# The filter's features for all positions first, then transformed by the forward's tiles, in a long convolution with a mixture of experts

## The chip, the cores and the metric

The kernel runs on one core of a Trainium2 chip. The metric is the device time of one execution in microseconds (us), as the median of several runs. TensorE (PE) multiplies matrices into PSUM, VectorE (DVE), ScalarE (ACT) and GpSimd (POOL) do the elementwise work, and SyncE (SP) issues nearly all loads and stores. Each engine works through its own instructions in the order in which the program wrote them.

## The reference

Four sequences of 11456 positions with 128 channels are convolved with a long filter, gated, and sent through a mixture of eight experts:

```python
h_mlp = np.maximum(pos_emb @ w1, 0.0) @ w2          # (11456, 64) -> (11456, 128)
h_filt = h_mlp * np.exp(-0.01 * pos)[:, None]
u = x * v
L = 2 * S
y = np.fft.irfft(np.fft.rfft(u, n=L, axis=1) * np.fft.rfft(h_filt, n=L, axis=0)[None], n=L, axis=1)[:, :S]
x = (x * y).reshape(B * S, D)
logits = x @ w_gate + modality_bias[modality_id]
e_idx = np.argmax(logits, axis=1)                   # one expert of 8 for each token
out[mask] = gate_w[mask, None] * (np.maximum(x[mask] @ w1[e], 0.0) @ w2[e])
```

Only `pos_emb`, `w1` and `w2` enter the filter, which is the same for all four sequences.

## The kernel before

The Fourier transforms are products with constant matrices. A position is split into a block (2 of them), a place n and its mirror (the two "ways"), and one of N2 = 64 remainders. A forward transform first makes the even and the odd part of the two ways, multiplies them with `fwd` (90 columns, over n), and then, in the middle stage, with matrices `c_to` over the 64 remainders. The middle stage runs over NM = 23 groups g of up to four of the 90 frequencies.

The first stage (0 to about 75 us) has 16 quarters q of two kinds. For sequence 0, `load(q)` fetches 512 KB of x (`xd`) and 512 KB of v, `product(q)` on DVE multiplies them and makes the even and odd parts (three instructions, in place in v's buffer), and `transform(q)` multiplies with `fwd`: two halves of 16 matmuls, each half into one of two PSUM pairs, from which ACT copies into the tile `A`. For the filter, `load(q)` fetches 256 KB of `pos_emb`, `hidden(q)` multiplies with w1 (four matmuls), DVE applies the relu and the window, and `transform(q)` multiplies at once with `whole`, a matrix that does even, odd and `fwd` together (four matmuls of 128x180); ACT copies to the tile `B`, which shares its memory with work buffers.

The middle stage of sequence 0 has more to do than the others, since the filter is finished in it: `turn(g)` transposes four 128x128 tiles of `B` on TensorE, and ACT copies them out; `analysis(g)` multiplies with `c_to`; `second(g)` multiplies with w2; `keep(g)` stores the spectrum of the filter for the sequences that follow. `swap(g)` (ACT), `spectrum(g)` (PE, then DVE and POOL) and `inverse(g)` (PE, ACT) belong to the sequence. Then follow the inverse transform, routing, and the experts, which the change leaves alone.

The order on every engine is written by the class `Timeline`: each piece has a time (a number without unit), and all pieces are issued in the order of time, place and rank. The tables `FOUT`, `FIRST` and `MID0` give the offset of each piece: `turn:-3` means that `turn(g)` stands three groups ahead of the sequence's `spectrum(g)`. A load waits until its buffer is free, and SP waits with it; so whatever is behind it on SP waits too. `ring_of` lists the buffers of each name.

Lines in the profile: L506 and L509 are `hidden`, L519 and L523 the filter's `transform`, L471, L474 and L475 `product`, L486 and L489 the sequence's `transform`, L561 and L562 `turn`, L570 and L574 `analysis`, L584 to L590 `second`, L599 and L600 `swap`, L617 to L644 `spectrum`, L658 and L662 `inverse`.

Of the kernel before, what the change touches and what calls it, by code (L numbers as in the profile page):

```python
# [91 lines left out]
def shape_constants():  # L92
# [6 lines left out]
    whole = np.zeros((2, 64, N1, 2))  # L99
    whole[:, :HALF, :, 0], whole[0, :HALF, :, 1], whole[1, :HALF, :, 1] = even, odd, -odd  # L100
# [22 lines left out]
    win = win.reshape(2, 64, 2, N2).transpose(2, 1, 3, 0)  # L123
# [18 lines left out]
        "c_inv": f(inv.reshape(N1, D)), "c_to": f(to), "c_back": f(back), "c_early": f(np.concatenate([win.reshape(D, 2 * N2), whole.reshape(D, 2 * N1)], 1)),  # L142
# [36 lines left out]
def hyena_moe_kernel(ctx: ExitStack, tc: tile.TileContext, a: dict, out: bass.AP,  # L179
# [184 lines left out]
    with ExitStack() as cv:  # L364
# [13 lines left out]
        early = bs2.rearrange("p o e c -> p (o e c)")[:, 0:2 * N2 + 2 * N1]  # L378
        win = early[:, 0:2 * N2].rearrange("p (q m) -> p q m", q=NQ)
        whole = early[:, 2 * N2:2 * N2 + 2 * N1]  # L380
# [4 lines left out]
        def first_constants():  # L385
            sp.dma_start(wf, a["wf"].rearrange("p (a d) -> p a d", a=2))
            act.dma_start(early, a["c_early"])
            act.dma_start(fwd, a["c_fwd"].rearrange("p (c m) -> p c m", c=2))
            act.copy(warm[:, 1:2], warm[:, 0:1])
# [36 lines left out]
        spare = bs2.rearrange("p o e c -> p (o e c)")  # L426
        aT_t, z_t = spare[:, 0:U // 2], spare[:, U // 2:U]
        B = work[:, 6 * U:6 * U + N1 * D].rearrange("p (k m) -> p k m", k=N1)

# [27 lines left out]

        def forward_stages(b):
            kept = {}

            def load(q):
                if q == 0:
                    from_first("seq")
                for name in ("xd", "v"):
                    t = kept[q, name] = ring("seq" if b else "seq0")
                    sp.dma_start(t, a[name][b, q])

            def product(q):

                u, e = kept.pop((q, "xd")), kept.pop((q, "v"))  # L470
                paced(dve.tensor_mul(u, u, e))  # L471
                e = kept[q, "e"] = e.rearrange("p (c m) -> p c m", c=2)
                u = u.rearrange("p (w m) -> p w m", w=2)
                dve.tensor_add(e[:, 0], u[:, 0], u[:, 1])  # L474
                paced(dve.tensor_sub(e[:, 1], u[:, 0], u[:, 1]))  # L475

            def transform(q):

                e = kept.pop((q, "e")).rearrange("p c (j n) -> p c j n", n=N2)
                for h in range(2):  # L480
                    p = pair("s1")
                    for j in range(4):
                        for c in range(2):
                            for blk in range(2):
                                at = slice(64 * blk, 64 * blk + 64)
                                pe.matmul(p[64 * c:64 * c + 64, blk, N1 * j:N1 * j + N1],  # L486
                                          e[at, c, 4 * h + j], fwd[at, c], start=True, stop=True)
                    d0 = 8 * q + 4 * h
                    act.copy(A[:, :, :, d0:d0 + 4],  # L489
                             p[:, :, 0:4 * N1].rearrange("p b (n k) -> p b k n", n=4))  # L490

            return load, product, transform

        def filter_stages():

            kept = {}

            def load(q):
                t = kept[q, "emb"] = ring("emb")
                sp.dma_start(t, a["pos_emb"][q])  # L500

            def hidden(q):
# [5 lines left out]
                r = ring("r").rearrange("p (m f) -> p m f", m=8)  # L508
                dve.scalar_tensor_tensor(  # L509
                    r, m1.rearrange("p (m f) -> p m f", m=8), 0.0,  # L510
                    win[:, q].unsqueeze(2).broadcast_to([D, 8, D // 2]),
                    op0=ALU.max, op1=ALU.mult)
                kept[q, 1] = r.rearrange("p (n b) f -> p n (b f)", b=2)

            def transform(q):
                r = kept.pop((q, 1))
                p = pair("s1")
                for j in range(4):
                    pe.matmul(p[:, j // 2, 2 * N1 * (j % 2):2 * N1 * (j % 2 + 1)],  # L519
                              r[:, j], whole, start=True, stop=True)  # L520
                for h in range(2):
# [10 lines left out]
        def middle_stages(b):  # L532
# [24 lines left out]
            def turn(g):  # L557
                n = 2 * kept[g]["n"]
                pa = bank("pa")
                for j in range(n):  # L560
                    pe.transpose(pa[:, D * j:D * j + D], B[:, 4 * g + j], ident)  # L561
                act.copy(aT_t[:, 0:n * D], pa[:, 0:n * D])  # L562

            def analysis(g):
# [6 lines left out]
                z = z_t.rearrange("p (t c s k) -> p t c s k", t=2, c=2, s=2)  # L571
# [4 lines left out]
            def second(g):  # L576
                n = kept[g]["n"]
                z = z_t.rearrange("p (t c m) -> p t c m", t=2, c=2)
# [87 lines left out]
            return todo if b else dict(todo, turn=turn, analysis=analysis, second=second, keep=keep)  # L666
# [219 lines left out]
        line.stages(0, NQ, FOUT, filter_stages())  # L886
        line.stages(0, NQ, FIRST, dict(zip(("load", "product", "forward"), forward_stages(0))))
        at = NQ + 3
# [23 lines left out]
        line.put(4, constants, 9)  # L912
        line.put(9, split_constants, 9)
# [259 lines left out]
def device_inputs(inputs):  # L1173
# [3 lines left out]
    for name, of, lay in (("x", "x", tile4), ("xd", "x", tile8), ("v", "v", tile8)):  # L1177
# [5 lines left out]
        pos.transpose(3, 0, 5, 4, 2, 1).reshape(NQ, D, -1))  # L1183
# [28 lines left out]
```

## Time and profile before

| | us |
|---|---|
| median of 3 runs | 2187.88 (2186.36 to 2192.39) |
| the profiled execution | 2187.52 |
| its span | 2185.7 |
| PE, DVE, ACT, POOL busy in the span | 2072.5, 1755.0, 1314.2, 979.8 |

The span is the time from the first to the last instruction; around it lie 1.8 us. PE is busy for 95% of it, but this is an average over stages with different limits. Of the chain that ended last, PE holds 78%, DVE 8%, ACT 3% and DMA 2%.

The change touches the first 235 us: the first stage, to about 75 us, and the middle stage of sequence 0, to about 235 us. Everything after is the same code in the same order.

### The profile page before, as it was taken

Reading aid. Unit: us, or ns where it says so; the run is one execution under the profiler, and the core shown is the slowest. Engines: PE = TensorE matmul, PEld = TensorE weight load, DVE = VectorE, ACT = ScalarE, POOL = GpSimd, SP = SyncE. Lnnn points to the kernel's source line nnn. Section 1 sums busy time; section 2 is a strip of 40 time slices with the busy share of each in tenths; the row PEclk is TensorE's granted clock in tenths of the full one; section 3 lists DMA queues with packets and bytes.
Section 4 is the critical chain, followed back from the end, with each engine's and each line's share of the span. In section 5 each row is a group of like instructions: output and inputs, shape, how many; then the busy total and the mean of one; then the engine's idle time right before and its main releaser. Section 6 shows DMA issues by size and latency. Waiting matters only on the chain.

```text
span 2185.7 us, 48874 instructions
## 1 busy us (share of the span) xinstructions
PE 2072.5 (95%) x18002; PEld 1632.5 (75%) x18002; DVE 1755.0 (80%) x2789; ACT 1314.2 (60%) x2451; POOL 979.8 (45%) x905
## 2 busy tenths in 40 slices
PE   8999898999889998999899999999999999999997
PEld 7787664776557665775578888887888888888897
DVE  7677897998889888986677777778777777777796
ACT  4555574456634665455556666666666666666685
POOL 0133003775568555865555666633333333333332
PEclk9999998999999999999899999999999999999999
DMA  9454677879878898856776222212111111111111
GB/s 373 139 157 145 220 264 225 258 259 307 297 244 267 281 307 257 281 190 194 210 235 191 82 77 80 75 57 63 41 48 47 43 48 43 48 47 42 40 41 30
DMA packets 195405, 341.59 MB, mean 156 GB/s; under 512 B 32785, under 2 KB 116077, under 8 KB 195161
## 3 DMA queue, kind: packets, MB, share of 16 engines
q1 hardware_dynamic: 171769, 290.82, 41.6%
q0 software_dynamic: 23104, 47.34, 6.6%
q8 instruction: 144, 2.36, 0.4%
q14 instruction: 100, 0.82, 0.1%
q10 hardware_dynamic: 288, 0.25, 0.0%
HBM read 253.87 MB, written 84.83 MB: 155 GB/s over the span
## 4 chain that ended last, share of the span: by engine, by line
PE 78%; DVE 8%; issue 6%; ACT 3%; DMA 2%; POOL 1%; SPq 1%; another core or an unknown queue 0%; DVEq 0%; POOLq 0%; ACTq 0%
PE pw L658 8%; PE ph L1067 7%; PE ph L1065 7%; PE ph L1066 7%; PE po L1091 7%; PE po L1089 7%; PE po L1090 7%; PE pz L617 6%; PE py L691 5%; PE wt L682 4%; PE s L486 3%; PE xT L740 2%; PE pt L1103 2%; PE px L1048 2%; PE pl L748 1%
## 5 line engine op out<-in xcount | busy, mean ns | idle before, releaser
L1071 DVE SCALAR_TENSOR_TENSOR hl<-ph,hh 128x512 fp32r<-128x512 f32 x724 | 498.8, 689 | 229.9 <-ACT hh L1070 176.1
L1070 ACT ACTIVATE hh<-ph 128x512 fp32r<-128x512 f32 x724 | 434.5, 600 | 371.5 <-PE ph L1067 329.0
L1113 POOL DMA_INDIRECT out<-ot,idx x362 | 368.4, 1018 | 578.5 <-DVE hl L1071 427.6
L272 POOL DMA_INDIRECT xs<-back,to x360 | 390.3, 1084 | 378.8 <-DVE sc L781 111.5
L1089 PE MATMUL po<-hh,wh 128*128 128x512 f32 (+1 forms) x792 | 303.9, 384 | 3.1 <-ACT hh L1070 3.1
L1065 PE MATMUL ph<-xh,wh 128*128 128x512 f32 (+1 forms) x792 | 304.5, 384 | 2.0 <-ACT wh L1036 2.0
L1091 PE MATMUL po<-hl,wh 128*128 128x512 f32 (+1 forms) x792 | 296.0, 374 | 0.9 <-DVE hl L1071 0.9
L1067 PE MATMUL ph<-xl,wh 128*128 128x512 f32 (+1 forms) x792 | 296.2, 374 | 0.5 <-DVE xl L1052 0.4
L1066 PE MATMUL ph<-xh,wl 128*128 128x512 f32 (+1 forms) x792 | 294.9, 372 | 0.0
L1090 PE MATMUL po<-hh,wl 128*128 128x512 f32 (+1 forms) x792 | 294.7, 372 | 0.0
L662 ACT COPY A<-pw 128x512 f32<-128x512 f32 (+1 forms) x184 | 97.0, 580 | 185.3 <-PE pw L658 185.3
L617 PE MATMUL pz<-A,work 128*64 128x256 f32 x1440 | 182.6, 397 | 7.2 <-DMA work<-in_c_to 6.3
L658 PEld LDWEIGHTS pw<-work 64*128 64x128 f32 x2856 | 166.4, 190 | 25.7 <-ACT work L599 14.2
L627 POOL TENSOR_TENSOR work<-work 128x512 f32<-128x512 f32 (+1 forms) x92 | 115.2, 1252 | 152.0 <-DVE work L623 151.8
L658 PE MATMUL pw<-work 64*128 64x128 f32 x2856 | 178.5, 278 | 0.0
L1091 PEld LDWEIGHTS po<-hl,wh 128*128 128x128 f32 x792 | 149.3, 189 | 29.4 <-DVE hl L1071 2.2
L1067 PEld LDWEIGHTS ph<-xl,wh 128*128 128x128 f32 x792 | 149.6, 189 | 28.3 <-DVE xl L1052 1.2
L1089 PEld LDWEIGHTS po<-hh,wh 128*128 128x128 f32 x792 | 149.5, 189 | 26.5 <-ACT hh L1070 3.8
L1065 PEld LDWEIGHTS ph<-xh,wh 128*128 128x128 f32 x792 | 149.8, 189 | 25.9 <-ACT wh L1036 2.4
L1066 PEld LDWEIGHTS ph<-xh,wl 128*128 128x128 f32 x792 | 150.1, 190 | 24.4 <-DVE wl L1037 0.4
L1090 PEld LDWEIGHTS po<-hh,wl 128*128 128x128 f32 x792 | 149.9, 189 | 23.3
L691 PE MATMUL py<-work,inv 90*64 90x512 f32 x512 | 139.2, 623 | 17.3 <-issue 6.5
(176 smaller groups left out, 3678.0 us busy)
## 6 DMA issues: line engine op xcount, KB each, us to landing
work<-hs SPq DMA_DIRECT2D x66, 512.0 KB
work<-in_x SPq DMA_DIRECT2D x64, 512.0 KB
work<-in_xd SPq DMA_DIRECT2D x54, 512.0 KB
work<-in_v SPq DMA_DIRECT2D x54, 512.0 KB
xr<-xo SPq DMA_DIRECT2D x64, 365.6 KB
back<-xr SPq DMA_DIRECT2D x120, 195.0 KB
work<-in_c_to SPq DMA_DIRECT2D x88, 256.0 KB
x<-xs SPq DMA_DIRECT2D x82, 260.0 KB
```

The costliest lines, as they stand in the source:

```text
L272: s = pool.indirect_dma_start(out=xs, out_offset=bass.IndirectOffsetOnAxis(ap=ix, axis=0), in_=src, in_offset=None, bounds_check=E * R - 1 ...
L617: pe.matmul(z[64 * s:64 * s + 64, t, r], k["b"][:, t, s, r], A[:, :, 4 * g + 2 * t + s], start=True, stop=True)
L658: pe.matmul(v[s][:, t, blk], k[of][at, t, r, blk], k["c"][at, t, r], start=i == 0, stop=i == len(terms) - 1)
L1065: pe.matmul(p, k[0, "h"][:, f:f + D], k["xh"], start=True, stop=False)
L1066: pe.matmul(p, k[0, "l"][:, f:f + D], k["xh"], start=False, stop=False)
L1067: pe.matmul(p, k[0, "h"][:, f:f + D], k["xl"], start=False, stop=True)
L1070: act.activation(hh, ph, AF.Relu)
L1071: steps.append(ins_of(dve.scalar_tensor_tensor(hl, ph, 0.0, hh.bitcast(F32), op0=ALU.max, op1=ALU.subtract)))
L1089: pe.matmul(po, k[1, "h"][:, f], hh[:, t], start=g == 0, stop=False)
L1090: pe.matmul(po, k[1, "l"][:, f], hh[:, t], start=False, stop=False)
L1091: pe.matmul(po, k[1, "h"][:, f], hl[:, t], start=False, stop=g == NCH - 1)
L1113: s = pool.indirect_dma_start(out=out, out_offset=bass.IndirectOffsetOnAxis(ap=ix, axis=0), in_=src, in_offset=None, bounds_check=N - 1, o ...
```

## The change

All of the filter's 16 `hidden` pieces come first. Their result, for every q, is made even and odd by two POOL instructions (an add and a subtract, 128x256 each) into a tile of features, `feat`, which lies in the memory of `A`. The layout of `pos_emb` is changed on the host so that the two ways of a position stand in one partition. Then eight `transform(k)` pieces, each with eight features, go through `quarters`, the same code as the sequence's `transform`. The result stands in `B` as `analysis` reads it, so `turn` is gone, and `analysis(g)` stands at -3 instead of -2. Since `feat` lies in `A`, no `transform` of the sequence can be issued before the filter's last.

The tables `FOUT` and `FIRST` become one table `FIRST` with times: emb(q) at q - 4, hidden(q) at q, transform(k) at 17 + k, product(q) at 5.5, 11.5, 16.5, 18.5 and so on, forward(q) at 26 + 2q, load(q) at 2, 8, 11, 12, 13, 16.7, 18.7, and then 12.2 + 2q. Ten buffers in a row (xd and v mixed) become three for xd and seven for v. `z` gets two buffers.

```diff
-FOUT = "hidden:1 transform:3 load:-2"
-FIRST = "product:3 forward:4 load:0"
-MID0 = ("inverse:2 swap:0 spectrum:0 second:-1 analysis:-2 turn:-3 load_c:-1 keep:0 load:-4")
+FIRST = {
+    "hidden": lambda q: q, "emb": lambda q: q - 4, "transform": lambda k: NQ + 1 + k,
...
+MID0 = ("inverse:2 swap:0 spectrum:0 second:-1 analysis:-3 load_c:-1 keep:0 load:-4")
...
-                ("h0", [flat(t)[:, 0:2 * U] for t in xo_t]),
-                ("seq0", [flat(t)[:, k * U:k * U + U] for t in xo_t for k in range(2)]
-                 + [work[:, i * U:i * U + U] for i in range(4)])):
+                ("h0", [flat(xo_t[i])[:, 0:2 * U] for i in (1, 2, 0)]),
+                ("xd0", [work[:, i * U:i * U + U] for i in range(3)]),
+                ("v0", [flat(t)[:, k * U:k * U + U] for t in xo_t for k in range(2)]
+                 + [work[:, 3 * U:4 * U]])):
...
+        feat = A.rearrange("p b k d -> p (b k d)")[:, 0:8 * U].rearrange(
+            "p (k c j n) -> p k c j n", k=8, c=2, j=8)
...
+        def quarters(e, of, d0):
+
+            for h in range(2):
+                p = pair("s1")
+                for j in range(4):
+                    for c in range(2):
+                        for blk in range(2):
+                            at = slice(64 * blk, 64 * blk + 64)
+                            pe.matmul(p[64 * c:64 * c + 64, blk, N1 * j:N1 * j + N1],
+                                      e[at, c, 4 * h + j], fwd[at, c], start=True, stop=True)
+                d = d0 + 4 * h
+                act.copy(of[:, :, :, d:d + 4],
+                         p[:, :, 0:4 * N1].rearrange("p b (n k) -> p b k n", n=4))
...
-            def transform(q):
-                r = kept.pop((q, 1))
-                p = pair("s1")
-                for j in range(4):
-                    pe.matmul(p[:, j // 2, 2 * N1 * (j % 2):2 * N1 * (j % 2 + 1)],
-                              r[:, j], whole, start=True, stop=True)
-                for h in range(2):
-                    n0 = 4 * q + 2 * h
-                    act.copy(B.rearrange("p k (c n) -> p (k c) n", c=2)[:, :, n0:n0 + 2],
-                             p[:, h, 0:4 * N1].rearrange("p (n k) -> p k n", n=2))
+                r = r.rearrange("p (n w k j) -> p w k j n", n=4, w=2, k=8)
+                for c, f in enumerate((pool.tensor_add, pool.tensor_sub)):
+                    f(feat[:, :, c, :, 4 * q:4 * q + 4], r[:, 0], r[:, 1])
+
+            def transform(k):
+                quarters(feat[:, k], B.rearrange("p k (b f) -> p b k f", b=2), 8 * k)
...
-            def turn(g):
-                n = 2 * kept[g]["n"]
-                pa = bank("pa")
-                for j in range(n):
-                    pe.transpose(pa[:, D * j:D * j + D], B[:, 4 * g + j], ident)
-                act.copy(aT_t[:, 0:n * D], pa[:, 0:n * D])
-
...
-                    pe.matmul(pz[:, at], aT_t[:, at], of[:, at], start=True, stop=True)
+                    pe.matmul(pz[:, at], B[:, 4 * g + j], of[:, at], start=True, stop=True)
...
-        at = NQ + 3
+        for rank, (name, when) in enumerate(FIRST.items()):
+            for q in range(8 if name == "transform" else NQ):
+                line.put(when(q), lambda f=todo[name], q=q: f(q),
+                         2 if name in ("emb", "load") else 0, rank, q)
+        at = 53.5
```

Line numbers move with it: L506 and L509 become L511 and L514, the matmuls and copies of `quarters` are L468 and L471, the POOL adds L520, `product` L487 to L491, the loads L482 (xd, v) and L505 (`pos_emb`), `analysis` L562, `second` L577, `spectrum` L610, `inverse` L651. In the rows of the order, a count such as x16 counts instructions; the trace counts every f32 matmul twice.

On PE, in the first stage, before: one period of the 16, where `m` is `hidden`, `s` a PSUM pair, `xo` and `back` buffers of the sequence and of the features.

```order
L519 MATMUL s_220<-bs_123,back 128x180 x4
L506 MATMUL m_237<-wf,work 128x128 x4
L486 MATMUL s_243<-fwd,xo_92 64x90 x16
L486 MATMUL s_261<-fwd,xo_92 64x90 x16
L519 MATMUL s_279<-bs_123,back 128x180 x4
```

On PE, in the same stage now: the last two `hidden`, and the first of the filter's transforms, which read `A`.

```order
L511 MATMUL m_277<-wf,work 128x128 x4
L511 MATMUL m_285<-wf,work 128x128 x4
L468 MATMUL s_298<-fwd,A 64x90 x16
L468 MATMUL s_316<-fwd,A 64x90 x16
L468 MATMUL s_334<-fwd,A 64x90 x16
```

Where filter and sequence took turns, 16 `hidden` pieces stand first, then 16 halves of the filter, then the sequence.

On SP, before, in the middle of the first stage: `pos_emb` of one quarter, and x and v of the sequence, in turn.

```order
L500 DMA work<-in_pos_emb 128x512
L466 DMA work<-in_xd 128x1024
L466 DMA work<-in_v 128x1024
L500 DMA work<-in_pos_emb 128x512
L466 DMA xo_91<-in_xd 128x1024
L466 DMA xo_91<-in_v 128x1024
```

On SP now, behind the constants: load(6), load(7), whose v goes into the buffer (`xo_91`) that forward(0) reads, and load(8) behind it.

```order
L482 DMA work<-in_xd 128x1024
L482 DMA work<-in_v 128x1024
L482 DMA work<-in_xd 128x1024
L482 DMA xo_91<-in_v 128x1024
L482 DMA work<-in_xd 128x1024
L482 DMA xo_91<-in_v 128x1024
```

All of `pos_emb` stands ahead of these rows now. From `xo_91<-in_v` on, every load of v stands behind a forward transform on PE, and SP's later issues behind it.

On PE, before, at the end of the first stage: the last filter transform, the last forward, then the middle stage's first pieces (`pa` is the turn, `pz` an analysis, `pq` a `second`).

```order
L519 MATMUL s_976<-bs_123,back 128x180 x4
L486 MATMUL s_984<-fwd,xo_91 64x90 x16
L486 MATMUL s_1002<-fwd,xo_91 64x90 x16
L561 MATMUL pa<-ident,work 128x128 x4
L570 MATMUL pz<-work,bs_123 128x128 x4
L561 MATMUL pa<-ident,work 128x128 x4
L584 MATMUL pq<-wf,bs_123 128x128 x8
L570 MATMUL pz<-work,bs_123 128x128 x4
L561 MATMUL pa<-ident,work 128x128 x4
L617 MATMUL pz<-A,work 64x256 x8
```

On PE now, at the same place: the end of forward(13), the first analysis, forward(14), an analysis, the first `second`, an analysis, forward(15), and the first `spectrum`.

```order
L468 MATMUL s_1137<-fwd,work 64x90 x16
L562 MATMUL pz<-work 128x128 x4
L468 MATMUL s_1164<-fwd,xo_91 64x90 x16
L468 MATMUL s_1182<-fwd,xo_91 64x90 x16
L562 MATMUL pz<-work 128x128 x4
L577 MATMUL pq<-wf,bs_123 128x128 x8
L562 MATMUL pz<-work 128x128 x4
L468 MATMUL s_1230<-fwd,xo_91 64x90 x16
L468 MATMUL s_1248<-fwd,xo_91 64x90 x16
L610 MATMUL pz<-A,work 64x256 x8
```

Before, all forward transforms stood ahead of the first `analysis`; now three analyses stand ahead of forward(15), and the first needs a load (`c_to`) that SP issues after all of the sequence's.

## Rows read from the trace of the kernel before

**Rows 1.** Chain that ended last, first stage, one period: start, us, engine and line

```profile
44.64 1.49 PE s L519 x8
46.13 0.89 PE m L506 x8
47.02 0.82 PE s L486 x32
47.87 0.77 ACT A L489
```

**Rows 2.** Chain that ended last, middle stage of sequence 0, one group

```profile
137.98 2.40 PE pw L658 x32
140.38 1.88 PE pz L617 x16
142.26 1.09 PE pq L584 x16
143.35 1.09 PE pz L570 x8
144.44 0.44 PE pa L561 x4
```

**Rows 3.** Timeline, DVE and ACT, middle stage: idle before and releaser in brackets

```profile
82.15 1.22 DVE L623 TENSOR_TENSOR work<-pz,xo 128x1024 f32<-128x1024 f32 x1 [2.10 <-PE pz L617]
88.75 1.22 DVE L623 TENSOR_TENSOR work<-pz,xo 128x1024 f32<-128x1024 f32 x1 [1.25 <-PE pz L570]
...
218.34 1.22 DVE L623 TENSOR_TENSOR work<-pz,xo 128x1024 f32<-128x1024 f32 x1 [1.55 <-ACT xo L600]
223.78 0.63 ACT L599 ACTIVATE xo<-xo 128x512 f32<-128x512 f32 x1 [0.83 <-DVE xo L590]
225.01 1.23 DVE L623 TENSOR_TENSOR work<-pz,xo 128x1024 f32<-128x1024 f32 x1 [1.32 <-ACT xo L600]
```

**Rows 4.** Groups by line and shape, POOL: busy us, mean ns, idle

```profile
L627 POOL TENSOR_TENSOR work<-work 128x512 f32<-128x512 f32 x88 | 112.3, 1276 | 140.1 <-DVE work L623 139.9
L627 POOL TENSOR_TENSOR work<-work 128x256 f32<-128x256 f32 x4 | 2.9, 726 | 11.9 <-DVE work L623 11.9
```

**Rows 5.** Timeline, PE and DVE, the first 13 us

```profile
4.99 3.68 PE L506 MATMUL m<-wf,work 128*128 128x128 f32 x16 [4.99 <-DMA work<-in_pos_emb]
7.07 0.69 DVE L509 SCALAR_TENSOR_TENSOR back<-m,bs 128x512 f32<-128x512 f32 x1 [6.19 <-PE m L506]
9.71 1.22 DVE L471 TENSOR_TENSOR xo<-xo 128x1024 f32<-128x1024 f32 x1 [0.31 <-DMA xo<-in_v]
11.58 0.69 DVE L475 TENSOR_TENSOR xo<-xo 128x512 f32<-128x512 f32 x1
```

**Rows 6.** Windows: PE, PEld, DVE, ACT, POOL busy, granted clock, DMA share, GB/s

```profile
20.00:30.00 10.00, 9.22 (x178) 8.47 (x171) 8.17 (x11) 5.52 (x10) 0.00 (x0) 1.00 1.02 377
30.00:40.00 10.00, 9.48 (x224) 8.77 (x227) 7.54 (x13) 5.54 (x11) 0.00 (x0) 1.00 1.03 405
40.00:50.00 10.00, 9.22 (x188) 8.45 (x178) 8.12 (x11) 5.72 (x10) 0.00 (x0) 1.00 1.03 404
```

**Rows 7.** Timeline, SP and DVE, loads into an idle queue

```profile
230.95 0.51 SPq L593 DMA_DIRECT2D hs<-xo  x1
...
232.70 0.38 SPq L466 DMA_DIRECT2D work<-in_v  x1
...
238.39 1.22 DVE L471 TENSOR_TENSOR work<-work 128x1024 f32<-128x1024 f32 x1 [1.13 <-DMA work<-in_v]
```

**Rows 8.** Windows of 2 us, columns as in rows 6

```profile
228.00:230.00 2.00, 0.21 (x3) 0.24 (x4) 1.86 (x3) 0.00 (x0) 0.00 (x0) 1.00 0.00 0
230.00:232.00 2.00, 1.90 (x18) 1.60 (x18) 1.16 (x4) 0.71 (x2) 0.00 (x0) 0.50 0.00 0
232.00:234.00 2.00, 1.72 (x18) 1.53 (x16) 1.97 (x3) 0.25 (x1) 0.73 (x1) 0.65 0.96 287
```

More of the change, by code (lines that the diff above doesn't have):

```diff
@@ L63 @@
 TAIL = NQ + 3
-FOUT = "hidden:1 transform:3 load:-2"
-FIRST = "product:3 forward:4 load:0"
-MID0 = ("inverse:2 swap:0 spectrum:0 second:-1 analysis:-2 turn:-3 load_c:-1 keep:0 load:-4")
+FIRST = {
+    "hidden": lambda q: q, "emb": lambda q: q - 4, "transform": lambda k: NQ + 1 + k,
+    "product": lambda q: (5.5, 11.5)[q] if q < 2 else 12.5 + 2 * q,
+    "forward": lambda q: 26 + 2 * q,
+    "load": lambda q: (2, 8, 11, 12, 13, 16.7, 18.7)[q] if q < 7 else 12.2 + 2 * q}
+MID0 = ("inverse:2 swap:0 spectrum:0 second:-1 analysis:-3 load_c:-1 keep:0 load:-4")
 MID = "swap:0 spectrum:0 inverse:2 load_c:-1 load:-3"
@@ L141, in shape_constants @@
         "c_fwd": f(fwd.reshape(D, 2 * N1)),
-        "c_inv": f(inv.reshape(N1, D)), "c_to": f(to), "c_back": f(back), "c_early": f(np.concatenate([win.reshape(D, 2 * N2), whole.reshape(D, 2 * N1)], 1)),
+        "c_inv": f(inv.reshape(N1, D)), "c_to": f(to), "c_back": f(back), "c_win": f(win.reshape(D, 2 * N2)),
         "c_small": f(small), "c_pad": f(pad.reshape(D, -1)),
@@ L386, in first_constants @@
             sp.dma_start(wf, a["wf"].rearrange("p (a d) -> p a d", a=2))
-            act.dma_start(early, a["c_early"])
+            act.dma_start(win.rearrange("p q m -> p (q m)"), a["c_win"])
             act.dma_start(fwd, a["c_fwd"].rearrange("p (c m) -> p c m", c=2))
@@ L464, in load @@
                 for name in ("xd", "v"):
-                    t = kept[q, name] = ring("seq" if b else "seq0")
+                    t = kept[q, name] = ring("seq" if b else name + "0")
                     sp.dma_start(t, a[name][b, q])
@@ L477, in transform @@
             def transform(q):
-                e = kept.pop((q, "e")).rearrange("p c (j n) -> p c j n", n=N2)
-                for h in range(2):
-                    p = pair("s1")
-                    for j in range(4):
[L483 to L490, printed above, removed]
+                quarters(kept.pop((q, "e")).rearrange("p c (j n) -> p c j n", n=N2), A, 8 * q)
             return load, product, transform
@@ L507, in hidden @@
                               start=True, stop=True)
-                r = ring("r").rearrange("p (m f) -> p m f", m=8)
+                r = ring("r")
                 dve.scalar_tensor_tensor(
-                    r, m1.rearrange("p (m f) -> p m f", m=8), 0.0,
+                    r.rearrange("p (m f) -> p m f", m=8), m1.rearrange("p (m f) -> p m f", m=8), 0.0,
                     win[:, q].unsqueeze(2).broadcast_to([D, 8, D // 2]),
                     op0=ALU.max, op1=ALU.mult)
-                kept[q, 1] = r.rearrange("p (n b) f -> p n (b f)", b=2)
-            def transform(q):
-                r = kept.pop((q, 1))
-                p = pair("s1")
-                for j in range(4):
-                    pe.matmul(p[:, j // 2, 2 * N1 * (j % 2):2 * N1 * (j % 2 + 1)],
-                              r[:, j], whole, start=True, stop=True)
-                for h in range(2):
-                    n0 = 4 * q + 2 * h
-                    act.copy(B.rearrange("p k (c n) -> p (k c) n", c=2)[:, :, n0:n0 + 2],
-                             p[:, h, 0:4 * N1].rearrange("p (n k) -> p k n", n=2))
+                r = r.rearrange("p (n w k j) -> p w k j n", n=4, w=2, k=8)
[3 more added lines that the diff above has]
+                quarters(feat[:, k], B.rearrange("p k (b f) -> p b k f", b=2), 8 * k)
             return dict(hidden=hidden, transform=transform, load=load)
@@ L665, in middle_stages @@
             todo = dict(inverse=inverse, spectrum=spectrum, load_c=load_c, load=load, swap=swap)
-            return todo if b else dict(todo, turn=turn, analysis=analysis, second=second, keep=keep)
+            return todo if b else dict(todo, analysis=analysis, second=second, keep=keep)
         def inverse_stages(b):
@@ L885, in hyena_moe_kernel @@
         line = Timeline()
-        line.stages(0, NQ, FOUT, filter_stages())
-        line.stages(0, NQ, FIRST, dict(zip(("load", "product", "forward"), forward_stages(0))))
-        at = NQ + 3
+        todo = filter_stages()
+        todo["emb"] = todo.pop("load")
+        todo |= zip(("load", "product", "forward"), forward_stages(0))
+        for rank, (name, when) in enumerate(FIRST.items()):
[3 more added lines that the diff above has]
+        at = 53.5
         for b in range(nb + 1):
@@ L911, in hyena_moe_kernel @@
             dve.memset(used, 0.0)
-        line.put(4, constants, 9)
-        line.put(9, split_constants, 9)
+        line.put(18, constants, 9)
+        line.put(30, split_constants, 9)
         line.run()
```

19 lines of the change are left out of this document (8 added, 11 removed).

## The prediction, made before the changed kernel ran

> **What bounds the kernel now.** I read the chain that ended last first, in the two stretches that the change touches, then the timeline of DVE and ACT there, then the windows for the DMA rate and the clock.
>
> In the first stage the chain repeats every 4.04 us: the filter's transform on PE, `hidden`, one half of the forward, and ACT's copy of that half, which frees a PSUM pair [rows 1]. So a quarter costs PE time and one trip through ACT. DMA is saturated next to it, at 377 to 405 GB/s [rows 6], mean 395, but it runs ahead into ten buffers and is not in this chain.
>
> In the middle stage of sequence 0 the chain is PE alone: 2.40 + 1.88 + 1.09 + 1.09 + 0.44 = 6.90 us for a group, of which the turn is 0.44 [rows 2]. Close behind PE stands a ring of two other engines: DVE's `spectrum` (L623) to the end of its `second` (L590), ACT's swap (L599, L600), and L623 of the next group. Where PE did not set the pace, that ring did: from 82.15 to 88.75, 6.60 us, and from 218.34 to 225.01, 6.67 us, where L599 waited for DVE's L590 [rows 3]. The reader is to see that 6.90 has a floor of some 6.65 under it. From the first L623 at 82.15 to the 22nd at 225.01 are 21 steps in 142.86 us, 6.80 each.
>
> **The change part by part.** I follow one event, the first L623 (82.15 before), then the 21 steps to the 22nd; after that the program is the same and moves along.
>
> *Features first.* The first `hidden` and its DVE instruction come as before, 7.07 + 0.69 [rows 5], so POOL starts its adds at 7.85. There are 32 adds of 128x256. An add of this size and type costs 0.73 us [rows 4], all its operands contiguous. The new ones read with a step of 128 elements and write runs of four, which no row shows. From below, two adds cost 1.30 us for a quarter (0.73 less some overlap of queued instructions); from above I take the row of twice the size, 1.28 each, 2.55 for a quarter. The nearest row is 0.73, and I take 1.6 for a quarter, its double with 0.14 for the hand-over and the steps.
>
> [...]
>
> Six quarters then end at 17.5. But DVE's queue has product(0) ahead of the seventh. Its v is issued behind emb(6), which waits for `hidden(2)`, and that ends about 9.8 (3.68 us for the first two from 4.99, one more at about 1.1) [rows 5]. What a load costs beyond its bytes I take from the four transfers from 230.95 to 232.70: a store of 256 KB and three loads of 512 KB, 1.84 MB, 4.6 us at 395 GB/s; DVE had the last at 238.39, 7.4 after the first issue [rows 7]. So 2.8 us are fixed. Emb(6), xd(0) and v(0) are 1.31 MB, 3.3 us: landed at 15.9. Product(0) takes 2.56 us (9.71 to 12.27 [rows 5]), to 18.5, then the DVE instruction of quarter 6, 0.69, and POOL resumes at 19.3. Ten quarters at 1.6 end at 35.3. Product(1) fits in between.
>
> *The filter's transforms.* Before, 16 of 1.49 us on PE [rows 1]. Now eight quarters, 16 halves on two PSUM pairs, and a pair comes back after 0.82 + 0.77 and 0.06 of issue, 1.65 for two halves [rows 1]: 13.2 us. They start after PE has waited from about 28 to 35. [...] PE holds 0.82 of each 1.65 with the copies as cover, so I charge 1.4. The last filter transform is done at 49.9.
>
> *The loads behind it.* `feat` lies in `A`, so forward(0) comes only then, and ends its reading 1.5 us later, at 51.4. The seven v buffers are full by then: all of `pos_emb` and seven pairs are 11.5 MB, 29 us at 395 GB/s, so DMA stands idle for some time before 51.4, and v(7) waits for forward(0). From there v(7) and eight pairs are 17 transfers of 512 KB, 8.91 MB, 22.6 us at 395 GB/s, with 2.8 fixed: v(15) lands at 76.8. The first c_to, 256 KB, stands behind it: 77.5. The forwards before it are hidden: from 49.9, 14 at 1.65 end at 73.0.
>
> *The way into the middle stage.* analysis(0) waits for c_to. Then PE has analysis, forward(14), analysis, second, analysis, forward(15): 4 x 1.09 and 2 x 1.47 (two halves with PE not waiting for pairs, 0.65 + 0.82), 7.3; the last copy 0.77, `spectrum` 1.88, hand-over 0.1. L623 starts at 87.5. Against 82.15 this is +5.3 us, which the overlap of analyses and forwards already serves to shorten.
>
> *The middle stage.* PE loses 0.44 a group, to 6.46; but the ring of DVE and ACT keeps its 6.60 to 6.67, so what is late next is L623. 21 steps at 6.65 are 139.7 against 142.9: -3.2 us, not -9.
>
> *At nothing.* ACT's turn copies go, but ACT is not in the chain there; c_to must be there a group earlier, 7.5 us after its buffer is freed (1.09 + 1.09 + 2.40 + 1.88 + 1.09 of PE [rows 2]), and needs 2.8 fixed and 2.7 for the 1.05 MB of a group's stores and loads, 5.5; were it 2 us later, PE would wait in every group. The smaller first constants, two z buffers and the later split constants lie beside other work.
>
> *Sum.* 5.3 - 3.2 = +2.1 on the profiled 2187.52 (span 2185.7 and 1.8 around it); the median of the runs is 0.36 above the profiled time: 2190.0.
>
> **The rivals.**
>
> *POOL is slower, and is blocked (slower).* Place: the 32 adds. At 1.0 us an add, between the two rows of 0.73 and 1.28 [rows 4], a quarter costs 2.0, and if the two products of this phase and POOL exclude each other, twice 2.56 us more: 7.85 + 32.0 + 5.1 = 45.0 instead of 35.3, and everything up to the first L623 moves by +9.7, to 2199.7. It decides against me from 2.0 us a quarter without blocking (+4.5), or from 1.7 with it. For it: a layout that no row shows. Against: the same op, type and count at 0.73, and in the middle stage POOL keeps 1.28 throughout [rows 4]. [...]
>
> *The ring is shorter and PE sets the pace (faster).* L623 could come at PE's 6.46: 21 x 0.19 = -4.0. With adds at 1.30 a quarter (-3.0), no lower clock (-1.4) and loads at 405 GB/s (-0.6), 2181.0. For it: the rows of 6.60 and 6.67 are from the stage's two ends. Against: L599 waits for L590 there, and both stay where they are.
>
> *The loads are hidden after all.* Were v(7) issued early enough, PE would go from 49.9 through 16 forwards at 1.65, four pieces of 1.09, 0.77, 1.88 and 0.1: L623 at 83.4, -4.1, 2185.9. Against it: its buffer is one that forward(0) reads.
>
> **How the numbers follow.** A measurement of this kernel tells 0.3%, 6.6 us, from no change; that is 2181.3 to 2194.5. My forecast has 0.38 and the hidden loads 0.06, both within; the slow POOL 0.36, with all between 2194.5 and its bound; the fast case 0.20. The slow rival has nearly my forecast's chance, but it needs two things that no row shows. The bounds: two adds at 2.55 give 7.85 + 40.8 = 48.7, +13.4, 2203; the fast case 2181. I leave out the ends and say 2182 to 2201; the forecast's own range is 2185 to 2194. Faster 0.20, the same 0.44, slower 0.36.
>
> **What would show it.** In the changed kernel: POOL's adds (L520) at 0.7 to 0.9 us, the first `quarters` matmul on PE at about 35; a lower granted clock behind it; DMA idle for some us up to 51 and saturated from there to 77; the first analysis (L562) waiting for c_to; L616, the former L623, first at 87 and then every 6.6 to 6.7 us with the swap waiting for DVE. I am wrong if the adds take 1.0 or more, if DMA has no gap, if PE does not wait for c_to, or if the steps are 6.5 or 6.9.

## The result, and the profile after

The changed kernel takes 2211.4 us in the median of four runs (2206.88 to 2214.68), against 2187.12 us of the kernel before beside it (2184.97 to 2192.39): a ratio of 1.0106, 95% interval 1.008 to 1.0132. It is slower by some 24 us, where +2.1 was forecast, which would not have been told from no change. The profiled execution is the lowest of the four, 2206.88 us (span 2205.1).

The event that the prediction followed, the first L616 (before: L623), starts at 109.89 instead of 82.15, against a forecast of 87.5; the 22nd at 250.18 instead of 225.01 [rows 3]. So the whole loss has happened by the start of the middle stage. Split at the forecast's own marks, times in us (the start of the first filter transform is that of its main run; four rows of it ran at 45.43):

| | forecast | measured | missed by |
|---|---|---|---|
| first filter transform on PE | 35.3 | 46.89 | +11.6 |
| from there to the first analysis | 42.2 | 52.8 | +10.6 |
| from there to the first L616 | 10.05 | 10.2 | +0.15 |
| 21 steps of L616 | 139.7 | 140.3 | +0.6 |

The chain that ended last, in the first stage of the changed kernel (start, us, engine and line):

```profile
7.10 39.75 POOL A L520 x32
46.89 2.69 PE s L468 x60
...
60.60 0.89 PE s L468 x32
61.52 0.77 ACT work L471
62.33 0.89 PE s L468 x32
...
67.96 0.69 PE s L468 x22
68.65 2.19 issue
...
98.60 1.16 PE s L468 x47
99.76 1.09 PE pz L562 x8
```

Two pieces are new against [rows 1]: 39.75 us of POOL alone, and stops named "issue", in which PE waits for nothing that the profile shows. From 60.60 to 62.33 the forecast's period is there, PE, ACT's copy and the hand-over; it takes 1.73, with 0.89 on PE, where 1.65, with 0.82, was charged.

POOL's group, and DVE beside it (start, us, engine, line, idle before and releaser):

```profile
L520 POOL TENSOR_TENSOR A<-back 128x256 f32<-128x256 f32 x32 | 39.7, 1280 | 5.7 <-DVE back L514 5.7
```

```profile
11.30 0.69 DVE L514 SCALAR_TENSOR_TENSOR back<-m,bs 128x512 f32<-128x512 f32 x1 [0.30 <-POOL A L520]
13.36 0.69 DVE L514 SCALAR_TENSOR_TENSOR back<-m,bs 128x512 f32<-128x512 f32 x1 [1.37 <-POOL A L520]
15.42 2.03 DVE L487 TENSOR_TENSOR work<-work,xo 128x1024 f32<-128x1024 f32 x1 [1.37 <-DMA xo<-in_v]
17.48 1.44 DVE L490 TENSOR_TENSOR xo<-work 128x512 f32<-128x512 f32 x1
...
47.31 1.21 DVE L487 TENSOR_TENSOR work<-work,xo 128x1024 f32<-128x1024 f32 x1
48.55 0.69 DVE L490 TENSOR_TENSOR xo<-work 128x512 f32<-128x512 f32 x1
```

Where no product runs, L514 waits for POOL and comes every 2.06 us, so an add takes 1.03, not the 0.8 charged from [rows 4]. Where a product runs, both suffer: L487 takes 2.03 instead of 1.21, L490 1.44 instead of 0.69, and an add up to 2.05; the mean of all 32 adds is 1.28. Four products run beside adds: DVE reaches products 2 and 3 at 38.11 and 42.40, while POOL, late by then, still works until 46.84. PE waits 15.3 us meanwhile.

PE's timeline in the forwards:

```profile
67.96 0.69 PE L468 MATMUL s<-fwd,xo 64*64 64x90 f32 x22 [0.27 <-ACT A L471]
70.84 1.09 PE L468 MATMUL s<-fwd,xo 64*64 64x90 f32 x42 [2.19 <-issue]
72.21 1.51 PE L468 MATMUL s<-fwd,xo 64*64 64x90 f32 x64 [0.28 <-ACT A L471]
73.99 0.68 PE L468 MATMUL s<-fwd,xo 64*64 64x90 f32 x21 [0.27 <-ACT A L471]
76.26 1.55 PE L468 MATMUL s<-fwd,xo 64*64 64x90 f32 x43 [1.59 <-issue]
```

and PE's waits from 30 to 100 us (total, times, longest):

```profile
PE s L468 <- POOL A L520: 16.2, 2, 15.3
PE s L468 <- issue: 9.0, 7, 2.2
PE s L468 <- ACT A L471: 2.2, 8, 0.3
```

The same before, from 15 to 75 us, all lines:

```profile
PE s L519 <- ACT A L489: 3.4, 13, 0.3
PE s L486 <- ACT work L523: 0.2, 1, 0.2
```

PE waits neither for DVE nor for DMA in the changed kernel's forwards, so these are not short of products or buffers. The counts tell what the stops may be. From one to the next lie 42 + 64 + 21 = 127 matmul rows; the later gaps are 43 + 64 + 20, 44 + 64 + 19, 109 + 18 and 110 + 17, all 127. With as many weight loads that is some 254 instructions. Of the two DMA queues named "instruction", q8 moved 146 packets and 2.39 MB in the whole run, and PE has 36,592 instructions, 251 for a packet of 16.4 KB. (Before: 144 packets for 36,004, 250 each.) The DMA view in steps of 0.25 us has one packet of q8 at 68.5, 73.75, 78.25, 85.0, 91.25 and 96.0, and PE goes on 2 to 3 us behind each of them. The profile does not say what PE waits for there. The author's reading, from these counts and times, is that PE stops at the end of each fetched block of its own program; the runs without and with more loads, below, test whether the stops go with the loads. In the changed kernel's forwards such a block lasts 5.0 to 6.3 us from stop to stop (70.84, 76.26, 81.32, 87.35, 93.65, 98.60: mean 5.55). At the pace of two quarters, 2 x 1.79, it would last 3.6; from 51.5 to 62.0, with DMA idle for most of the time, the packets come every 3.5 us. Before, one period of 4.04 us held 8 + 8 + 32 + 32 = 80 rows [rows 1], so a block lasted some 6.4 us (q8's ten packets from 18.5 to 73.0 are 6.1 apart). At that pace none of PE's waits was a stop, though loads ran at 377 to 405 GB/s [rows 6].

Windows of the forwards (columns as in [rows 6]):

```profile
64.00:74.00 10.00, 6.51 (x257) 5.44 (x258) 4.72 (x6) 5.86 (x10) 0.00 (x0) 1.00 0.89 321
74.00:84.00 10.00, 7.65 (x252) 6.95 (x256) 7.52 (x12) 5.42 (x8) 0.00 (x0) 0.83 0.93 336
84.00:94.00 10.00, 5.86 (x179) 5.14 (x172) 7.91 (x10) 4.06 (x6) 0.00 (x0) 0.82 0.85 303
```

Against [rows 6] PE is busy for 5.9 to 7.7 us of ten, not 9.2 to 9.5, and the mean granted clock falls to 0.82: in windows of 2 us it is at 0.50 from 78 to 80, 88 to 90 and 94 to 96, each time behind a stop (1.59, 2.19 and 1.49 us). DMA moves less, since SP waits for buffers, 3.8 us for forwards and 9.7 for products in these 30 us.

The middle stage (L616 on DVE) answers to [rows 3]:

```profile
109.89 1.22 DVE L616 TENSOR_TENSOR work<-pz,xo 128x1024 f32<-128x1024 f32 x1 [4.06 <-PE pz L610]
...
156.47 1.23 DVE L616 TENSOR_TENSOR work<-pz,xo 128x1024 f32<-128x1024 f32 x1 [1.32 <-ACT xo L593]
163.14 1.22 DVE L616 TENSOR_TENSOR work<-pz,xo 128x1024 f32<-128x1024 f32 x1 [1.32 <-ACT xo L593]
...
250.18 1.23 DVE L616 TENSOR_TENSOR work<-pz,xo 128x1024 f32<-128x1024 f32 x1 [1.32 <-ACT xo L593]
```

From the second on it waits for ACT's swap each time, and comes every 6.60 to 6.67 us but once (7.04): the ring that was named as the floor.

### The profile page after: what moved, and what is told of

Read it like the earlier page. It is cut to its first block, busy times and chain, and to the rows that moved or that the text cites. A ratio compares the mean times of both kernels' runs of the same rounds, so it can differ in the third digit from the quotient of the medians.

```text
span 2205.1 us, 49450 instructions
## 1 busy us (share of the span) xinstructions
PE 2057.4 (93%) x18296; PEld 1622.8 (74%) x18296; DVE 1763.1 (80%) x2789; ACT 1302.8 (59%) x2412; POOL 1020.8 (46%) x937
## 3 DMA queue, kind: packets, MB, share of 16 engines
q8 instruction: 146, 2.39, 0.4%
## 4 chain that ended last, share of the span: by engine, by line
PE 71%; DVE 12%; issue 8%; ACT 4%; POOL 3%; DMA 1%; SPq 1%; DVEq 0%; another core or an unknown queue 0%; POOLq 0%; ACTq 0%
PE ph L1065 7%; PE ph L1063 7%; PE po L1089 7%; PE ph L1064 7%; PE po L1087 7%; PE po L1088 7%; PE pw L651 6%; PE pz L610 5%; PE py L684 5%; PE wt L675 4%; PE s L468 4%; DVE work L625 3%; PE xT L733 2%; POOL A L520 2%; DVE work L616 2%
## 5 line engine op out<-in xcount | busy, mean ns | idle before, releaser
L610 PE MATMUL pz<-A,work 128*64 128x256 f32 x1440 | 183.2, 398 | 9.4 <-DMA work<-in_c_to 4.6
L651 PEld LDWEIGHTS pw<-work 64*128 64x128 f32 x2856 | 166.6, 190 | 26.1 <-ACT work L592 12.3
L651 PE MATMUL pw<-work 64*128 64x128 f32 x2856 | 178.6, 279 | 0.0
L625 DVE TENSOR_TENSOR work<-pz,work 128x2048 f32<-128x2048 f32 (+1 forms) x69 | 154.1, 2233 | 0.0
```

The lines of the kernel that those rows point to most:

```text
L610: pe.matmul(z[64 * s:64 * s + 64, t, r], k["b"][:, t, s, r], A[:, :, 4 * g + 2 * t + s], start=True, stop=True)
L651: pe.matmul(v[s][:, t, blk], k[of][at, t, r, blk], k["c"][at, t, r], start=i == 0, stop=i == len(terms) - 1)
```

## The experiments

Theory A: the adds and their contention with the products delay the filter's transforms. Theory F: behind them PE stops for its own instructions, which are fetched slowly beside saturated loads. Theory G, F's rival: PE stops there whatever the loads do. Theory H: a ring of DVE and ACT sets the middle stage's step. Chips differ by some 2% in the whole (the kernel before took 2142.99 to 2187.12 us in the median); every ratio is to the kernel before on the same chip, and times inside the first 250 us are compared directly. Where no ratio stands, the kernel ran once, and is read by its trace alone. Differences in round brackets are to the changed kernel.

**The adds read runs of neighbours** (and write with steps):

```diff
-                r = r.rearrange("p (n w k j) -> p w k j n", n=4, w=2, k=8)
+                r = r.rearrange("p (n w k j) -> p w n k j", n=4, w=2, k=8)
-                    f(feat[:, :, c, :, 4 * q:4 * q + 4], r[:, 0], r[:, 1])
+                    f(feat[:, :, c, :, 4 * q:4 * q + 4].rearrange("p k j n -> p n k j"), r[:, 0], r[:, 1])
```

> Same adds on GpSimd, but their access order is turned so that both reads run over 64 neighbouring elements and only the write steps. Theory A (the step of the reads makes an add 1.04 us instead of the 0.73 of the contiguous row before, and products on VectorE hold adds off): an undisturbed add falls to 0.73 to 0.80 us, 32 adds take about 31 us instead of 39.7, the filter's first transform comes at about 38 instead of 46.9, and the time falls by 6 to 9 us against the changed kernel. Rival B (the size and the hand-over of an add cost 1.04, whatever the access): adds stay at 1.04 to 1.08 and the first transform at 46 to 47. If the step of the write costs as much as that of the reads, the same as B.

Measured, the adds (min, median, max in ns) of the changed kernel and of this one:

```profile
L520 POOL TENSOR_TENSOR A<-back x32: 1038/1076/2050, 7.1 to 45.3; 128x256 f32<-128x256 f32 x32
L520 POOL TENSOR_TENSOR A<-back x32: 732/735/1717, 7.3 to 37.9; 128x256 f32<-128x256 f32 x32
```

The mean is 0.79 us, the first transform comes at 39.17 (-7.7), but the first L616 at 107.34 (-2.6), and the ratio is 1.0111 [1.0088, 1.0134]: the 6 to 9 us expected of the whole did not come. PE's stops grew to 14.0 us in eight, the longest 4.7. The step of the read costs POOL 0.3 us an add (1.04 against 0.73), as A says. POOL now stands idle for 13.7 us instead of 5.7, waiting for features. Of the time won, two thirds are lost again behind the first transform, which A alone does not explain.

**Products 0 and 1 behind the last feature.** They then read x of quarters 3 and 4, which changes the values and lets these two loads start ahead of the products:

```diff
-    "product": lambda q: (5.5, 11.5)[q] if q < 2 else 12.5 + 2 * q,
+    "product": lambda q: 15.2 + q / 10 if q < 2 else 12.5 + 2 * q,
```

> Products 0 and 1 are moved behind the last feature's VectorE instruction; nothing else. Theory A (a VectorE instruction with two operands in SBUF and a GpSimd add exclude each other): no add before about 34 us is stretched, products 0 and 1 no longer stand at 15 to 20 and 28 to 32 us, and the adds lose only what the products beside the last three features take, 2 to 5 us instead of some 7: the first transform at 42 to 45. Rival B (the adds are stretched by loads that write SBUF, not by products): the max of an add stays near 2.05 us at the places where loads are dense, and the first transform stays at 46 to 47.

Measured: 32 adds of 1.065 in the mean, none over 1.08, though `pos_emb` was landing beside them (PE waited for it for 10.6 us in the first 45), so these loads do not stretch them; first transform at 40.13 (-6.8, better than expected), first L616 at 108.21 (-1.7), stops of 10.8 us. On DVE one product started before POOL was done:

```profile
34.69 6.47 DVE L487 TENSOR_TENSOR work<-work,xo 128x1024 f32<-128x1024 f32 x1
41.19 0.69 DVE L490 TENSOR_TENSOR xo<-work 128x512 f32<-128x512 f32 x1
...
44.87 1.22 DVE L487 TENSOR_TENSOR work<-work,xo 128x1024 f32<-128x1024 f32 x1
```

So the four products beside the adds had cost POOL 6.5 us (39.75 less 32 x 1.04). Here a whole queue of adds went ahead, to 40.1, and the product was held for over 5 us.

**All adds on DVE:**

```diff
-                for c, f in enumerate((pool.tensor_add, pool.tensor_sub)):
+                for c, f in enumerate((dve.tensor_add, dve.tensor_sub)):
```

> All 32 adds go from POOL to DVE. If POOL's time for an add and its contention with the two products were the cause of the late first transform (theory A), DVE holds 0.69 + 2 x 0.35 to 0.45 for a quarter, 16 of them 22 to 25, and two products of 2.56: first transform at 34 to 38 instead of 46.9, no product stretched (L487 1.22), and the first L616 at 98 to 101. If the strides cost on every engine as on POOL (rival), an add on DVE takes 1.0, a quarter 2.7, and the first transform comes at 53 or later.

Measured: an add takes 0.69, not 0.35 to 0.45; the products keep 1.22 and 0.69; first transform at 41.99 (-4.9), first L616 at 107.11 (-2.8), not 98 to 101; stops of 10.3 us. The rival's 53 is excluded, A's 34 to 38 missed by the size of the add.

**No loads in the forwards:** x and v of quarters 7 to 15 of sequence 0 are not loaded.

```diff
-                    sp.dma_start(t, a[name][b, q])
+                    if b or q < 7:
+                        sp.dma_start(t, a[name][b, q])
```

> Leaves out the loads of x and v of quarters 7 to 15 of the first sequence (their buffers are used as they stand), all else as in the changed kernel. Theory F (in the stretch of the forward transforms, PE's stops put down to issue are its instructions, fetched by DMA behind the loads): PE's idle time put down to issue in that stretch falls from some 9 us to under 1.5, the clock stays at its upper level, and 16 forwards take 28 to 30 us (1.73 each) plus the four pieces of the middle stage: the first L616 at 96 to 98 instead of 109.9. Rival G (PE stops and slows because of its own pauses between quarters and the buffers, whatever DMA does): stops of 1.5 to 2.2 us stay.

Measured: first transform at 47.22, as in the changed kernel, first analysis at 90.23: 43.0 us for the stretch instead of 52.8; first L616 at 100.43 (-9.5), though not the 96 to 98 expected. Two windows of this kernel's forwards, and PE's waits for "issue" from 40 to 100 us:

```profile
64.00:74.00 10.00, 9.20 (x377) 7.77 (x373) 6.67 (x11) 8.36 (x12) 0.00 (x0) 1.00 0.02 5
74.00:84.00 10.00, 9.29 (x372) 7.60 (x360) 9.58 (x13) 8.63 (x12) 0.00 (x0) 1.00 0.02 6
```

```profile
PE s L468 <- issue: 2.1, 1, 2.1
```

In these windows PE runs the same instructions at a granted clock of 1.00, and the stretch has one stop instead of seven. That one ends at 56.23, in the filter's transforms, behind loads of v, for which a product still waited until 52.99; the forwards have none. Of the 9.8 us, 6.9 are stops (9.0 less 2.1); some 3 are left, which fit the changed kernel's clock, 0.83 and 0.82 in two windows of 10 us. G falls.

**Nine needless loads of 512 KB beside the filter's transforms:**

```diff
         line.put(18, constants, 9)
+        free = A.rearrange("p b k d -> p (b k d)")
+        for i in range(9):
+            line.put(20 + i / 10, lambda i=i: sp.dma_start(
+                free[:, (9 + i) * U:(10 + i) * U], a["v"][0, i]), 2)
```

> Adds nine loads of 512 KB that nothing needs, issued beside the filter's transforms (about 47 to 62 us), where the changed kernel's DMA is idle and PE stops for only 0.7 us in all. Theory F: stops of 0.5 to 2.2 us put down to issue appear at each second quarter in the filter's transforms, 2 to 5 us in all, and the first forward comes 2 to 5 us later than 62.3. Rival G: no stop there over 0.7 us, the first forward at 62 to 63, and only the later loads move if the nine are not through by then.

Measured: stops of 1.37, 2.52 and 0.56 us in the filter's transforms, where the changed kernel had 0.64; 14.7 in nine in all. The first forward comes at 68.60 (+6.3, somewhat more than expected), the first L616 at 118.03 (+8.1). Two of the stops:

```profile
56.05 1.01 PE L468 MATMUL s<-fwd,A 64*64 64x90 f32 x40 [1.37 <-issue]
62.24 4.54 PE L468 MATMUL s<-fwd,A 64*64 64x90 f32 x128 [2.52 <-issue]
```

From 59.73 to 62.24 PE does nothing. With no loads the stops go (2.1 us for 9.0), with more loads they come where there was next to none (4.45 for 0.64): so much of F holds from both sides. That PE waits there for its instructions rests on the counts and times above.

**Subtract on DVE, nine buffers for v:**

```diff
-                 + [work[:, 3 * U:4 * U]])):
+                 + [work[:, i * U:i * U + U] for i in (3, 4, 5)])):
-                for c, f in enumerate((pool.tensor_add, pool.tensor_sub)):
+                for c, f in enumerate((pool.tensor_add, dve.tensor_sub)):
```

> The subtract of each quarter goes from POOL to DVE, and the ring for v gets two more buffers (nine). If the adds cost because there are 32 of 1.04 on one engine (theory A), POOL holds 16 x 1.05, and DVE 0.69 + about 0.4 for a quarter, so PE's first filter transform comes at 29 to 31 instead of 46.9. If DVE and POOL shut each other out wholly, the move brings next to nothing: 16 x (1.04 + 0.4 + 0.69) + 5, first transform at 44 or later. Behind it: if PE's forwards are held by instruction fetches behind saturated loads (theory F), 52.8 us from the first transform to the first analysis hardly shrink and the first L616 (109.9 after) stands at 92 to 95; if the forwards only lost by waiting for the seven buffers of v (theory R), the nine cut the stretch to about 43 and L616 stands at 83 to 86. Time against before: 1.004 to 1.006 by A and F, 1.000 by A and R.

Measured: first transform at 37.38, between the 29 to 31 of A and the 44 of its rival; first analysis at 90.74 (53.4 us later), L616 at 100.94 (-9.0), ratio 1.0077 [1.0059, 1.0096]. POOL's 16 adds take 1.48 each beside DVE's, and the subtract 0.74 instead of 0.4, so half the adds do not cost half the time. The stretch behind has not shrunk, with 9.4 us of stops in it: F, not the buffers of v alone.

**One add left out of the middle stage:**

```diff
-                else:
+                elif b > 0:
                     dve.tensor_add(m0[:, :, 0], m0[:, :, 0], m0[:, :, 1])
```

> In the middle stage of sequence 0 the add of 128x1024 behind the second product of spectrum (L636) is left out, so part of the sum of sequence 0's spectrum is missing; all else is the changed kernel. If the ring of DVE and ACT sets the pace (theory H), it is 6.67 - 1.15 = 5.5 us, and the steps of L616 go to PE's 6.45 to 6.50: 21 steps in 135.5 to 136.5 instead of 140.3, and L616 waits for PE. If PE sets it at 6.67, the steps stay.

Measured: 21 steps in 124.07 us (110.66 to 234.73), 5.91 each; in the steady part 6.04, and PE then has no gap. Its inverse:

```profile
152.98 2.06 PE L651 MATMUL pw<-back,work 64*128 64x128 f32 x32
159.02 2.06 PE L651 MATMUL pw<-back,work 64*128 64x128 f32 x32
```

So H holds, and by more than expected: PE's own need without the turn is 6.04, not 6.46.

**That add on POOL instead**, with the subtract on DVE and nine buffers for v:

```diff
-                else:
+                elif b > 0:
                     dve.tensor_add(m0[:, :, 0], m0[:, :, 0], m0[:, :, 1])
+                else:
+                    pool.tensor_add(m0[:, :, 0], m0[:, :, 0], m0[:, :, 1])
```

> As x8_best, and in the middle stage of sequence 0 the add of 128x1024 behind the second product of spectrum (L636, 1.23 us on DVE) goes to POOL (about 2.5 us, by twice the 1.28 of 128x512). If the ring of DVE and ACT sets the 6.67 us of a group (theory H), it falls to 5.5, PE's 6.46 sets the pace, and 21 steps take 135.7 to 137 instead of 140.3: 3 to 4.5 us less in all than x8_best. If PE sets the 6.67 (rival), nothing changes. If POOL beside DVE stretches DVE's instructions with SBUF inputs, L616 takes 1.3 to 1.5 and the steps stay at 6.6 or grow.

Measured: L616 from 101.72 to the 22nd at 227.17, 125.45 for 21 steps against 139.93 with those two edits alone, and far below the 135.7 to 137 expected; ratio 1.0012 [1.0001, 1.0024]. PE's need had fallen from 6.90 to 6.04 us a group, and of these 0.86 the ring had let through 0.23 in the steady part (6.90 to 6.67). Over all 21 steps it was 0.12 (6.80 to 6.68), since the ring had set the first seven steps before, too (6.60 to 6.67).

**The same edit on the kernel before:**

> The kernel before the change, with the one edit of the last run: in sequence 0 the add of 128x1024 behind the second product of spectrum (L643) goes to POOL. First stage as before, first L623 at about 82.15. If DVE and ACT's ring set the pace of a group here too as soon as PE was quick (theory H), and PE's inverse is 2.40 instead of 1.99 only because the ring is late, PE's pieces are 1.99 + 1.88 + 1.09 + 1.09 + 0.44 = 6.49 and 21 steps take 136 to 137 instead of 142.9: 6 us less, ratio about 0.997. If PE's 6.90 is its own pace with the turn in it, the steps stay and the ratio is 1.000; if POOL's longer work makes inverse wait, it is over 1.001.

Measured: steady steps of 6.90 as before, though L623 now waits 2.81 us for ACT; only the first steps shrink, and 21 take 141.39 instead of 142.86; ratio 1.0009 [0.999, 1.0027]. With the turn in it, PE itself needs 6.90. On PE:

```profile
158.00 0.60 PE L561 MATMUL pa<-ident,work 128*128 128x128 f32 x4
158.53 2.47 PE L660 MATMUL pw<-back,work 64*128 64x128 f32 x32
```

The inverse next to the turn takes 2.47, without the turn 2.06 (above). So the turn cost PE not 0.44 but 0.86. Why its neighbour is slow stays open.

**The three edits and the adds' runs together:**

> The changed kernel with subtract on DVE, nine buffers for v, the add of spectrum on POOL, and the features' adds reading runs of 64 neighbours. If the adds alone held the first transform (theory A), it comes 6 to 8 us earlier than 37.0, L616 at about 95, and the time is 0.997 to 0.998 of before. If the forwards behind it are held by instruction fetches behind saturated loads (theory F), the earlier start is given back there as it was with the runs alone: first transform at 30, L616 at 98 to 101, ratio 1.000 to 1.001.

Measured: first transform at 34.03 (not 30), first analysis at 91.18, L616 at 101.38, stops of 12.7 us; ratio 1.0017 [1.0, 1.0034]. Against the same kernel without the adds' runs (37.01 and 101.72), three microseconds won at the start arrive as 0.3: F's branch, if just beyond its upper end.

**x of the first quarters into the free part of `A`**, so that v gets ten buffers; on top of the last kernel, in two sizes. The core of the larger (ten quarters):

```diff
-                ("xd0", [work[:, i * U:i * U + U] for i in range(3)]),
+                ("xd0", [A.rearrange("p b k d -> p (b k d)")[:, i * U:i * U + U] for i in range(8, 18)]
+                 + [work[:, i * U:i * U + U] for i in (4, 5, 4, 5, 4, 5)]),
```

> As the last kernel (runs, split, POOL add), but x of quarters 0 to 7 is loaded into the part of A that feat leaves free, so v gets ten buffers and x and v of eight quarters stand in memory before the filter's transforms; only quarters 10 to 15 are still to be loaded once forward(0) has read its buffer. DVE must finish eight products before forward(0) may be copied to A. If the forwards are held by instruction fetches behind saturated loads (theory F) and by the late v (theory R), both go: first transform at 34 to 37, no stop for instructions in the filter's transforms, first analysis at 76 to 82, first L616 at 86 to 92 instead of 101.4, and the time is 0.993 to 0.997 of before. If the stops have nothing to do with the loads (rival), they stay at 11 to 13 us, L616 stays at 98 to 102 and the ratio at 1.000 to 1.002.

> The same with x of quarters 0 to 9 in A and four products before the last hidden. DVE must finish ten products before forward(0) may be copied: 6.4 + 16 x 1.3 + 10 x 2.56 = 53, against 48 with eight. By theory F the forwards then run with still less DMA beside them; first transform at 36 to 39, first L616 at 88 to 95, ratio 0.994 to 0.998. By the rival 98 to 104 and 1.000 to 1.003.

Measured, in the order above: first L616 at 97.98 and 99.22, ratios 0.9996 [0.9983, 1.0009] and 1.0008 [0.9996, 1.002]. In the smaller one products 8 to 13 read x of the quarter two further on, which changes values, and some of its waits too, so only the larger is read closely. Its stops are 6.8 us instead of 12.7, as F has it, but L616 gained 2 us, not 6 to 13, and the ratio shows none of the gain expected: DVE, with ten products to do first, and `pos_emb` behind more loads let the first transform come at 40.13. PE's timeline shows both cases in one kernel:

```profile
48.76 1.00 PE L469 MATMUL s<-fwd,A 64*64 64x90 f32 x39 [1.38 <-issue]
50.01 1.51 PE L469 MATMUL s<-fwd,A 64*64 64x90 f32 x64 [0.25 <-ACT work L472]
...
62.27 0.70 PE L469 MATMUL s<-fwd,xo 64*64 64x90 f32 x24 [0.21 <-ACT A L472]
65.15 4.61 PE L469 MATMUL s<-fwd,xo 64*64 64x90 f32 x127 [2.18 <-issue]
```

Between 48.76 and 65.15 lie 511 rows, four times some 128; at the three multiples between, within 50 to 60 us with DMA at a mean share of 0.07, PE does not stop, and the first one after the loads resume costs 2.18.

No version beats the kernel before by what can be measured; the best are level with it, and owe that to an edit that is not part of this change.

## Why the prediction was wrong

*Features first: failed in size, +11.6.* The add was charged at 0.8 from the contiguous row [rows 4]; it measured 1.03 to 1.06 undisturbed, and 0.73 once its reads ran over neighbours. That is 32 x 0.24 = 7.7 us. The rest is the mutual blocking of POOL and the products (a product's multiplication at 2.03 against 1.21, adds of up to 2.05 against 1.04), 6.5 us for four of them, where a gap of 1.8 for one was charged and the products at [rows 5] taken for undisturbed; POOL started 0.75 earlier than forecast: 7.7 + 6.5 - 1.8 - 0.75 = 11.6. The slow rival named both and put the first transform at 45.0; it was given less than the forecast because neither had a row.

*The filter's transforms: right in kind.* 15.4 us instead of 14.6, 0.64 of it a stop; the clock was granted at 0.50 from 34 to 48, with PE idle for 15.3 us up to 45.43. No run shows the 1.4 us charged for a slower clock: [rows 8] have 0.50 and 0.65 in the two windows of 2 us behind a nearly idle one, and here it was 0.50 up to 48, 0.62 from 48 to 50 and 1.00 from 50 to 76.

*The loads behind it: the step that failed, +10.6.* That v(7) waits for forward(0) was right (issued at 63.93, 1.6 us behind the filter's transforms, forecast 1.5). Wrong was "the forwards before it are hidden": 1.65 for a quarter was put together from parts of a stretch where PE used 80 matmul rows in 4.04 us, and carried over to one with 64 in 1.79. At that pace PE stopped after every 127 rows while DMA moved 303 to 336 GB/s; these stops, 8.4 us behind 62.33, read here as waits for its own program, stood in the sum at nothing. Product(15), which waits for v(15), then came 30.7 us behind v(7)'s issue, where v(15) was forecast to land 25.4 behind it, since late forwards free the buffers late; and the first analysis stood behind forwards on PE that were late, and did not wait for c_to, issued at 87.94. No rival had this; even the slow one's 2199.7 lacks it. What in the profile pointed to it: the "instruction" queue among the DMA queues, and a rate of instructions 1.8 times as high in the new order. Why PE stops that long beside loads, the runs do not show.

*The way into the middle stage and the middle stage: right.* 10.2 for 10.05, steps of 6.68 for 6.65, L616 waiting for the swap. "PE loses 0.44 a group, to 6.46" was wrong, it fell to 6.04. That did no harm, since the ring hid either; the term came out by its floor, not by PE's price.

*The sum.* +27.7 - 2.6 = +25.2 at the 22nd step, where +2.1 was forecast; the medians differ by 24.3.

## What to carry to other kernels

When work is regrouped by kind, count the instructions per microsecond of the new stretch, not only their durations: here a long run of 64x90 matmuls beside loads of 303 to 336 GB/s stood for 9.0 us in seven stops, and for 2.1 in one without those loads. For an elementwise instruction moved to POOL, look at its operands' steps and at the DVE instructions beside it, not at its shape alone: the same 128x256 add took 0.73 or 1.04 us by its steps, and up to 2.05 beside a product. And a stage with two limits close together pays back only the distance between them, until both are moved: here 0.23 us a group (6.90 to 6.67) of the 0.86 by which PE's need fell.

## What the runs showed of the hardware

- PE's stops in the forwards came every 127 matmul rows, some 254 instructions with the weight loads; the queue q8, named "instruction", moved a packet of 16.4 KB for every 251 of PE's instructions. Beside loads of 303 to 336 GB/s the stops ended 5.0 to 6.3 us apart (in the run with the adds' runs once 8.5), and with DMA nearly idle (a share of 0.02 to 0.07) PE did 127 rows in some 3.6 us without a stop.
- POOL adds of 128x256 f32: 1.04 us with a read step of 128 elements and runs of four written, 0.73 with reads in runs of 64 and stepped writes. On DVE the first form took 0.69, and 0.74 beside POOL's adds.
- A DVE multiplication with both inputs in SBUF (128x1024) took 6.47 us behind a queue of POOL adds (alone 1.22), and the adds stayed at 1.06; with adds on DVE and POOL at once, POOL's took 1.48.
